# GEGLU feed-forward on one core: the first loads and the first products in another order

## The chip, the cores and the metric

One Trainium2 chip, one of its cores. The metric is the device time of one execution in microseconds (us); lower is better. Engines: TensorE (PE, its weight loads PEld), VectorE (DVE), ScalarE (ACT), GpSimd (POOL), and SyncE (SP), which here only issues DMAs. ScalarE issues DMAs too; "ACTq" and "SPq" are the issues of the two.

## The reference

x is 2048 x 1024, w_gate and w_up are 1024 x 3584, w_down is 3584 x 1024, all bfloat16:

```
def _gelu(x):
    return jax.nn.gelu(x, approximate=True)

def reference(x, w_gate, w_up, w_down):
    return (_gelu(x @ w_gate) * (x @ w_up)) @ w_down
```

## The kernel before

The tokens are worked in two halves of 1024 (`NH`), each in two token blocks of 512 (`TB`). x is needed transposed: `xT[tb]` holds 8 row blocks (`KD`, index kd) of 128 features by 512 tokens. For each half the 28 feature chunks of 128 columns are taken in 14 pairs (`pair_quads`); gate and up products of a pair are made with fewer matmuls through sums and differences of blocks (`s_sum`, `t_sum`, a Strassen-Winograd scheme), and `down_group` does the same for w_down. gelu is on ScalarE, the product of gate and up on VectorE.

The very first pair of the first half is different, since neither x nor the weights are on the chip: `first_pair_units` multiplies directly, row block by row block (`part`, which calls `mm_gu`, L264). `j` is 0 for gate and 1 for up, `u` is the chunk of the pair. Token block 0 comes first, so its first products need only the first row blocks of x and of the weights:

- Row blocks 0 to 3 of x for token block 0 are loaded as they lie (`load_x0`; a "quarter" is two row blocks, 256 KB) and transposed on TensorE (`transpose_x0`, L308): quarter 0 gives blocks 0 and 1, quarter 1 gives blocks 2 and 3. They are copied out of PSUM by VectorE (L316), block 3 by ScalarE (L318).
- Row blocks 4 to 7, and the whole of token block 1, come through DMA transposes on SyncE's queue (`load_xT`, L171).
- The weights' first 256 columns (`FA`) are loaded in row blocks 0-1, 2-4 and 5-7 for gate and for up (`load_w`, L160), before the other columns. A row block of these is 64 KB.

Until the first x is there, TensorE runs `NWARM` = 7 matmuls on constants (`warm`, L202), and one more of half the width as a filler between the first transposes and the first products.

The order on each engine is written out by hand: `sp`, `act`, `dve`, `pool` and `pe` chain each instruction behind the last one on the same engine, so the order of the calls is the order on the engine and on its DMA queue. ScalarE's DMA issues, its table load (`preload_act_table`, L225) and its copies are thus in one line. The build gives DMA completions eight semaphores in turn, so that each DMA waits, on the issuing engine, for the landing of the DMA that stands eight before it in the order of issue. Before the change these waits are, in ScalarE's queue: gate rows 5-7 for the second half of x quarter 0, up rows 5-7 for x quarter 1.

Later, `x_fill` loads token block 0 of the second half from a transposed copy in DRAM, in two DMAs of 512 KB.

Of the kernel before, what the change touches and what calls it, by code (L numbers as in the profile page):

```python
# [34 lines left out]
def kernel(  # L35
# [8 lines left out]
    nc = tc.nc  # L44
    P = 128
# [4 lines left out]
    KD = D // P  # L50
    KH = KD // 2
    KF = F // P
    TB = 512
# [7 lines left out]
    TSB = TB // P  # L61
    XQ = 256
    NXQ = D // XQ
    KPQ = XQ // P
# [41 lines left out]
    banks = [psum.tile([P, TB], F32, name=f"bank{i}") for i in range(8)]  # L106
    PB, VB, QB, RB = (0, 1), (2, 3), (4, 5), (6, 7)
    last_on = {}

    def on(engine, inst):  # L110

        if engine in last_on:
            tc.add_manual_dep(
                inst.ins, last_on[engine].ins.name, SCHED_DEP, reason="engine order"
            )
        last_on[engine] = inst
        return inst

    def sp(inst):
        return on("sp", inst)  # L120
# [18 lines left out]
    def pe(inst):  # L139
        return on("pe", inst)  # L140
# [3 lines left out]
    chunks = {}  # L144
# [10 lines left out]
    def load_w(key, j, k0, k1, queue=sp, f0=0, f1=FG):  # L155

        c0 = key[1] * FG
        eng = nc.scalar if queue is act else nc.sync
        src = (wgv, wuv)[j][:, k0:k1, c0 + f0 : c0 + f1]
        queue(eng.dma_start(out=chunks[key][j][:, k0:k1, f0:f1], in_=src))  # L160

    def load_x0(q, queue, ts0=0, ts1=TSB):
        eng = nc.scalar if queue is act else nc.sync
        cols = slice(q * XQ, (q + 1) * XQ)
        src = x2[ts0 * P : ts1 * P, cols].rearrange("(ts p) d -> p ts d", p=P)
        queue(eng.dma_start(out=xs0[:, ts0:ts1, cols], in_=src))

    def load_xT(xT, h, tb, k0, k1):
        t0 = h * SH + tb * TB
        sp(  # L170
            nc.sync.dma_start_transpose(  # L171
                out=xT[tb][:, k0:k1, :],
                in_=xv[t0 : t0 + TB, k0:k1, :],
            )
        )

    def new_x(tb):
        xT[tb] = xT_pool.tile([P, KD, TB], BF16, name=f"xT{tb}")

    xT = [None] * NTB  # L180
# [4 lines left out]
    FA = 2 * P  # L185
    first = (0, 0)
    load_x0(0, sp, 0, 2)
    load_x0(0, act, 2, TSB)
    load_w(first, 0, 0, 2, sp, 0, FA)
    load_x0(1, act)  # L190
    load_w(first, 1, 0, 2, sp, 0, FA)
    load_w(first, 0, 2, 5, act, 0, FA)
    load_w(first, 1, 2, 5, sp, 0, FA)
    ident = const_pool.tile([P, P], BF16, name="ident")
    make_identity(nc, ident[:])

# [3 lines left out]
    def warm(bank, n=TB):  # L200
        pe(
            nc.tensor.matmul(  # L202
                banks[bank][:, 0:n],
                lhsT=warm_l,
                rhs=warm_r[:, 0:n],
                start=True,
                stop=True,
            )
        )
# [4 lines left out]
    load_xT(xT, 0, 0, KH, KH + 1)  # L214
    behind_transpose = last_on["sp"]
    load_xT(xT, 0, 0, KH + 1, KH + 2)
    for j in range(2):
        load_w(first, j, 5, KD, act, 0, FA)
        tc.add_manual_dep(
            last_on["act"].ins,  # L220
            behind_transpose.ins.name,
            SCHED_DEP,
            reason="engine order",
        )
# [16 lines left out]
    def t_sum(name, c0=0, c1=KH):  # L241
        def b(j, l):
            return xT[l][:, j * KH + c0 : j * KH + c1, :]

        t0 = ("t1", "t2", "t3", "b22", "t4").index(name) * KH * TB
        t = t_mem[:, t0 : t0 + KH * TB].rearrange("p (a b) -> p a b", b=TB)
        tsum[name] = t
        t = t[:, c0:c1, :]
        if name == "b22":
            for c in range(c1 - c0):  # L250
                act(nc.scalar.copy(out=t[:, c, :], in_=b(1, 1)[:, c, :]))
            return
        in0, in1 = {
            "t1": lambda: (b(0, 1), b(0, 0)),
            "t2": lambda: (b(1, 1), tsum["t1"].bitcast(F32)[:, c0:c1, :]),
            "t3": lambda: (b(1, 1), b(0, 1)),
            "t4": lambda: (b(1, 0), tsum["t2"].bitcast(F32)[:, c0:c1, :]),
        }[name]()
        dve(nc.vector.tensor_tensor(out=t, in0=in0, in1=in1, op=ALU.subtract))  # L259


    def mm_gu(ps, w_sb, fi, tb, kd):
        pe(
            nc.tensor.matmul(  # L264
                ps[:],
                lhsT=w_sb[:, kd, fi * P : (fi + 1) * P],
                rhs=xT[tb][:, kd, :],
                start=(kd == 0),
                stop=(kd == KD - 1),
            )  # L270
        )

# [23 lines left out]
    def unit_out(hT, bset, fi, tb):  # L296
        mult(hT, gelu(banks[bset[0]]), banks[bset[1]], fi, tb)

    def transpose_x0(q):

        parts = [(2 * q, 0, 4), (2 * q + 1, 0, 4)]
        if q == 0:
            parts = [(0, 0, 2), (0, 2, 4), (1, 0, 4)]
        for n, (kd, ts0, ts1) in enumerate(parts):
            tp = banks[(PB + QB)[(2 * q + n) % 4]][:].bitcast(BF16)
            for ts in range(ts0, ts1):
                pe(
                    nc.tensor.transpose(  # L308
                        tp[:, ts * P : (ts + 1) * P],
                        xs0[:, ts, kd * P : (kd + 1) * P],  # L310
                        ident[:],
                    )
                )
            cols = slice(ts0 * P, ts1 * P)
            if q == 0 or n == 0:
                dve(nc.vector.tensor_copy(out=xT[0][:, kd, cols], in_=tp[:, cols]))  # L316
            else:
                act(nc.scalar.copy(out=xT[0][:, kd, cols], in_=tp[:, cols]))  # L318

    def part(held, tb, k0, k1, us=(0, 1), js=(0, 1)):  # L320
        for kd in range(k0, k1):
            for j in js:
                for u in us:
                    mm_gu(banks[held[u][j]], chunks[first][j], u, tb, kd)

    def first_pair_units(hT):

        held = (VB, RB)
        transpose_x0(0)
        warm(RB[1], TB // 2)  # L330
        part(held, 0, 0, KPQ, js=(0,))
        transpose_x0(1)
        part(held, 0, 0, KPQ, js=(1,))
        part(held, 0, KPQ, KD)
        t_sum("t1", 0, KH // 2)
        t_sum("t1", KH // 2, KH)
        for u in range(2):
            unit_out(hT, held[u], u, 0)
        held = (QB, PB)
        part(held, 1, 0, KH)  # L340
        t_sum("t2")
        t_sum("b22")
        t_sum("t3", 0, KH // 2)
        part(held, 1, KH, KD, (0,))
        unit_out(hT, held[0], 0, 1)
        t_sum("t3", KH // 2, KH)
        part(held, 1, KH, KD, (1,))
        unit_out(hT, held[1], 1, 1)
        for j in range(2):
            s_sum(0, 1, j, "s3", True, False)  # L350
        for name in ("s1", "s2", "s4"):
            for j in range(2):
                s_sum(0, 1, j, name)
# [284 lines left out]
    def x_rows(k0, k1):  # L638
        return x_dram[k0:k1, :, :].rearrange("k p t -> p k t")
# [242 lines left out]
    for h in range(NH):  # L882
# [83 lines left out]
        if h + 1 < NH:  # L966
            nh = h + 1
            new_x(0)

            def x_fill():  # L970
                for k0, k1 in ((0, KH), (KH, KD)):
                    src = x_rows(k0, k1)
                    sp(nc.sync.dma_start(out=xT[0][:, k0:k1, :], in_=src))

            def w_fill(c, j):
                if j == 0:
                    new_chunk((nh, c))
                for k0 in range(0, KD, KH):
                    load_w((nh, c), j, k0, k0 + KH)

            def s_fill(j, *names):
                for name in names:
                    s_sum(nh, 0, j, name, True)

            then0["m6"] = [x_fill]
            then1["m6"] = [lambda: w_fill(0, 0)]
            then1["m7"] = [lambda: w_fill(0, 1)]
            then1["m2"] = [
                lambda: s_fill(0, "s1"),
                lambda: s_fill(1, "s1"),  # L990
                lambda: s_fill(0, "s2"),
                lambda: s_fill(1, "s2"),
                lambda: s_fill(0, "s3"),
                lambda: s_fill(1, "s3"),
            ]
            then1["m3"] = [lambda: t_sum("t1")]
            then1["m4"] = [
                lambda: s_fill(0, "a22"),
                lambda: s_fill(1, "a22"),
                lambda: t_sum("b22"),  # L1000
                lambda: t_sum("t2"),
                lambda: t_sum("t3"),
                lambda: s_fill(0, "s4"),
                lambda: s_fill(1, "s4"),
                lambda: t_sum("t4"),
                pool_behind_dve,
                lambda: [w_fill(1, j) for j in range(2)],
            ]
# [32 lines left out]
```

## Time and profile before

| | us |
|---|---|
| median of 5 runs | 539.63 |
| lowest and highest run | 539.58, 540.7 |
| the profiled execution, its own time | 539.1 |
| its span on the core | 537.3 |

| engine | busy, us | share of the span |
|---|---|---|
| TensorE matmul | 531.7 | 99% |
| TensorE weight load | 377.8 | 70% |
| VectorE | 363.0 | 68% |
| ScalarE | 263.3 | 49% |
| GpSimd | 243.1 | 45% |

A line of the timeline or of the chain reads: start in us from the span's start, duration in us, engine, line of the kernel, operation, out<-in, count, and in brackets the idle time of the engine just before and what ended it. "issue" in the chain is time in which nothing that the profile shows was waited for. Several instructions of one kind in a row are merged into one line, with the time from the first's start to the last's end. In the view by windows the columns after the engines are the granted TensorE clock, the mean busy share of the 16 DMA engines, and GB/s moved.

### The profile page before, as it was taken

The page shows a single profiled execution, that of the slowest core. Times are in us where ns is not written, and L with a number is a line of the kernel's source. Part 1 is how long each engine was busy: PE and PEld are TensorE (multiplying, and loading weights), DVE is VectorE, ACT ScalarE, POOL GpSimd, SP SyncE. Part 2 cuts the span into 40 slices and gives each one's busy share as a digit, 9 for nine tenths or more (in the row PEclk, how much of TensorE's full clock was granted, in tenths as well). Part 3 has the DMA queues.
Part 4 walks back from the last instruction along what each step waited for, and adds up shares of the span by engine and source line. Part 5 has one row for each costly group of instructions (what it writes and reads, how often), then busy time and mean ns, then how long its engine had stood idle before and what let it go on. Part 6 is the DMA issues. An engine that isn't in the chain of part 4 may idle for free.

```text
span 537.3 us, 7084 instructions
## 1 busy us (share of the span) xinstructions
PE 531.7 (99%) x2352; PEld 377.8 (70%) x2388; DVE 363.0 (68%) x476; ACT 263.3 (49%) x447; POOL 243.1 (45%) x212
## 2 busy tenths in 40 slices
PE   9999999999999999999999999999999999999997
PEld 4577776667776686777776677777777766866866
DVE  2988767778775997989674334444444469969961
ACT  2655555555555329117465555555555551452280
POOL 0699877777776000000066776667777730000000
PEclk9999999999999999999999999999999999999999
DMA  9946876697816967789940405042222448677846
GB/s 216 324 124 196 213 240 203 219 211 250 293 60 208 357 237 263 230 284 298 329 163 1 157 1 158 19 139 67 91 78 80 157 137 281 228 244 246 291 143 212
DMA packets 92547, 102.70 MB, mean 191 GB/s; under 512 B 18656, under 2 KB 67424, under 8 KB 92512
## 3 DMA queue, kind: packets, MB, share of 16 engines
q1 hardware_dynamic: 69568, 80.23, 46.4%
q10 hardware_dynamic: 22944, 22.02, 13.5%
q8 instruction: 19, 0.31, 0.3%
q14 instruction: 16, 0.13, 0.1%
HBM read 85.98 MB, written 12.58 MB: 183 GB/s over the span
## 4 chain that ended last, share of the span: by engine, by line
PE 99%; issue 0%; ACT 0%; ACTq 0%
PE bank L413 63%; PE bank L703 33%; PE bank L264 3%; PE bank L202 1%; PE bank L308 0%; ACT bank L468 0%; ACT o_sb L759 0%; ACTq L468 0%
## 5 line engine op out<-in xcount | busy, mean ns | idle before, releaser
L413 PE MATMUL bank<-t_mem,s_mem 128*128 128x512 f32 x1056 | 249.4, 394 | 0.0
L413 PEld LDWEIGHTS bank<-t_mem,s_mem 128*128 128x128 f32 x1056 | 198.2, 188 | 43.8 <-ACT bank L464 0.2
L385 POOL TENSOR_TENSOR s_mem<-w_mem 128x512 fp32r<-128x512 bf16 x102 | 119.9, 1199 | 191.2 <-DVE t_mem L259 102.7
L703 PE MATMUL bank<-t_mem,s_mem 128*128 128x512 f32 (+1 forms) x548 | 127.2, 391 | 0.0
L288 DVE TENSOR_TENSOR hT<-w_mem,bank 128x512 bf16<-128x512 f32 x104 | 71.2, 686 | 81.0 <-PE bank L413 45.7
L703 PEld LDWEIGHTS bank<-t_mem,s_mem 128*128 128x128 f32 x548 | 102.5, 188 | 22.0
L436 DVE TENSOR_TENSOR bank<-bank,m 128x512 f32<-128x512 f32 x108 | 69.9, 694 | 45.3 <-ACT m L458 43.6
L413 PE MATMUL bank<-xT,w_mem 128*128 128x512 bf16 x405 | 96.5, 380 | 1.4
L283 ACT ACTIVATE w_mem<-bank 128x512 f32<-128x512 f32 x104 | 61.8, 597 | 52.1 <-DVE bank L436 35.6
L413 PEld LDWEIGHTS <-w_mem 128*128 128x128 bf16 x432 | 40.2, 98 | 51.6 <-issue 6.8
L385 POOL TENSOR_TENSOR s_mem<-w_mem,s_mem 128x512 fp32r<-128x512 bf16 x52 | 65.7, 1290 | 0.0
L605 DVE TENSOR_TENSOR t_mem<-w_mem 128x1024 fp32r<-128x1024 bf16 x56 | 65.5, 1217 | 0.0
L385 POOL TENSOR_TENSOR s_mem<-s_mem,w_mem 128x512 fp32r<-128x512 f32 x52 | 60.8, 1195 | 0.0
L464 ACT COPY bank<-bank 128x512 f32<-128x512 f32 x54 | 30.8, 570 | 38.9 <-PE bank L413 38.9
L398 ACT CAST s_mem<-w_mem 128x512 fp32r<-128x512 bf16 x54 | 33.1, 615 | 31.5 <-PE bank L413 30.1
L675 DVE TENSOR_TENSOR s_mem<-hT 128x512 fp32r<-128x512 bf16 x52 | 34.2, 685 | 10.2 <-PE bank L703 9.4
L458 ACT COPY m<-bank 128x512 f32<-128x512 f32 x54 | 31.8, 589 | 17.5 <-PE bank L413 17.5
L703 PEld LDWEIGHTS <-hT 128*128 128x128 bf16 x224 | 21.3, 98 | 26.6 <-issue 2.1
L468 ACT COPY bank<-bank 128x512 f32<-128x512 f32 x54 | 30.7, 570 | 12.2 <-PE bank L413 12.2
L630 DVE TENSOR_TENSOR o_sb<-wd_sb,o_sb 128x512 fp32r<-128x512 bf16 x28 | 31.7, 1132 | 0.5
L768 ACT CAST o_sb<-bank 128x512 bf16<-128x512 f32 x27 | 14.8, 585 | 33.8 <-PE bank L703 33.8
L602 ACT CAST t_mem<-w_mem 128x1024 fp32r<-128x1024 bf16 x28 | 26.9, 1047 | 0.0
(45 smaller groups left out, 236.4 us busy)
## 6 DMA issues: line engine op xcount, KB each, us to landing
t_mem<-t_dram SPq DMA_DIRECT2D x56, 512.0 KB, 5.1
w_mem<-in_w_gate_dram ACTq DMA_DIRECT2D x10, 1024.0 KB, 5.3
w_mem<-in_w_up_dram ACTq DMA_DIRECT2D x10, 1024.0 KB, 5.5
wd_sb<-in_w_down_dram SPq DMA_DIRECT2D x28, 256.0 KB, 4.3
t_dram<-o_sb SPq DMA_DIRECT2D x28, 256.0 KB, 3.0
wd_sb<-in_w_down_dram SPq DMA_DIRECT2D x12, 512.0 KB, 7.7
w_mem<-in_w_down_dram SPq DMA_DIRECT2D x4, 1024.0 KB, 6.5
w_mem<-in_w_down_dram SPq DMA_DIRECT2D x8, 512.0 KB, 8.3
```

What stands on the lines that cost most here:

```text
L283: act(nc.scalar.activation(out=g_sb, in_=ps[:], func=ACT.Gelu_apprx_tanh))
L288: nc.vector.tensor_tensor(out=hT[:, fc, tb * TB : (tb + 1) * TB], in0=g_sb, in1=ps[:], op=ALU.mult,)
L385: pool(nc.gpsimd.tensor_tensor(out=t, in0=in0, in1=in1, op=op))
L398: act(nc.scalar.copy(out=t, in_=a(1, 1)))
L413: nc.tensor.matmul(banks[bank][:], lhsT=lhs[:, c, :], rhs=rhs[:, c, :], start=start and c == 0, stop=c == KH - 1, skip_group_check=True,)
L436: nc.vector.tensor_tensor(out=banks[dst][:], in0=banks[src][:], in1=m5[j][:], op=ALU.add)
L458: act(nc.scalar.copy(out=m5[j][:], in_=banks[V_[j]][:]))
L464: act(nc.scalar.copy(out=banks[RB[j]][:], in_=banks[QB[j]][:]))
L605: dve(nc.vector.tensor_tensor(out=t, in0=in0, in1=in1, op=ALU.subtract))
L630: dve(nc.vector.tensor_tensor(out=t, in0=in0, in1=in1, op=ALU.subtract))
L675: dve(nc.vector.tensor_tensor(out=t, in0=in0, in1=in1, op=op))
L703: nc.tensor.matmul(banks[bank][:, c0:c1], lhsT=lhs(i, u), rhs=rhs(i)[:, c0:c1], start=start and i == 0, stop=stop and i == NS - 1, skip_gr ...
```

## The change

The second x quarter is loaded in two halves by tokens, the first on ScalarE's queue and the second on SyncE's, where it stands before the up rows 0-1. Gate rows 2-4 stay on ScalarE's queue, now ahead of the point where the up loads are issued; up rows 2-4 go from SyncE's queue to ScalarE's, before gate and up rows 5-7. The filler matmul is gone; the gate products of row block 0 are made in two halves of 256 tokens each (the first half has `start`, the second writes other columns of the same bank). For row blocks 2 and 3 the gate products of both blocks come before the up products of both. `x_fill` is one DMA of 1 MB.

The waits for completion semaphores that the build gives ScalarE's queue are then: up rows 2-4 for the second half of x quarter 0, gate rows 5-7 for the first half of x quarter 1, up rows 5-7 for gate rows 2-4. The table load and the copy of row block 3 follow behind these issues, as before.

```
     load_x0(0, sp, 0, 2)
     load_x0(0, act, 2, TSB)
     load_w(first, 0, 0, 2, sp, 0, FA)
-    load_x0(1, act)
+    load_x0(1, act, 0, 2)
+    load_x0(1, sp, 2, TSB)
+    load_w(first, 0, 2, 5, act, 0, FA)
     load_w(first, 1, 0, 2, sp, 0, FA)
-    load_w(first, 0, 2, 5, act, 0, FA)
-    load_w(first, 1, 2, 5, sp, 0, FA)
...
     load_xT(xT, 0, 0, KH + 1, KH + 2)
-    for j in range(2):
-        load_w(first, j, 5, KD, act, 0, FA)
+    for j, k0, k1 in ((1, 2, 5), (0, 5, KD), (1, 5, KD)):
+        load_w(first, j, k0, k1, act, 0, FA)
         tc.add_manual_dep(
...
         transpose_x0(0)
-        warm(RB[1], TB // 2)
-        part(held, 0, 0, KPQ, js=(0,))
+        for t0 in (0, TB // 2):
+            for u in range(2):
+                pe(
+                    nc.tensor.matmul(
+                        banks[held[u][0]][:, t0 : t0 + TB // 2],
+                        lhsT=chunks[first][0][:, 0, u * P : (u + 1) * P],
+                        rhs=xT[0][:, 0, t0 : t0 + TB // 2],
+                        start=t0 == 0,
+                        stop=False,
+                        skip_group_check=True,
+                    )
+                )
+        part(held, 0, 1, KPQ, js=(0,))
         transpose_x0(1)
         part(held, 0, 0, KPQ, js=(1,))
-        part(held, 0, KPQ, KD)
+        for j in range(2):
+            part(held, 0, KPQ, KH, js=(j,))
+        part(held, 0, KH, KD)
...
             def x_fill():
-                for k0, k1 in ((0, KH), (KH, KD)):
+                for k0, k1 in ((0, KD),):
                     src = x_rows(k0, k1)
                     sp(nc.sync.dma_start(out=xT[0][:, k0:k1, :], in_=src))
```

More of the change, by code (lines that the diff above doesn't have):

```diff
@@ L329, in first_pair_units @@
         transpose_x0(0)
-        warm(RB[1], TB // 2)
-        part(held, 0, 0, KPQ, js=(0,))
+        for t0 in (0, TB // 2):
[7 more added lines that the diff above has]
+                        stop=False,
+                        skip_group_check=True,
+                    )
+                )
+        part(held, 0, 1, KPQ, js=(0,))
         transpose_x0(1)
         part(held, 0, 0, KPQ, js=(1,))
-        part(held, 0, KPQ, KD)
+        for j in range(2):
+            part(held, 0, KPQ, KH, js=(j,))
+        part(held, 0, KH, KD)
         t_sum("t1", 0, KH // 2)
```

## The prediction

> **What bounds the kernel now.** I read the page first, then the chain that ended last in order of time, then the first 20 us engine by engine, then the DMA issues one at a time. The page's busy shares and the chain's head:
>
> ```profile
> PE 531.7 (99%) x2352; PEld 377.8 (70%) x2388; DVE 363.0 (68%) x476; ACT 263.3 (49%) x447; POOL 243.1 (45%) x212
> ...
> 0.73 0.04 issue
> 0.77 3.14 PE bank L202 x7
> 3.92 0.84 PE bank L308 x8
> 4.76 0.11 PE bank L202
> 4.87 1.00 PE bank L264 x4
> 5.87 0.45 PE bank L308 x8
> 6.31 4.59 PE bank L264 x21
> 10.90 0.05 issue
> 10.96 8.36 PE bank L264 x38
> ```
>
> TensorE is the chain from its first matmul to 534.4 us. From 10.96 on a 512-column product takes 8.36 / 38 = 0.22 us, and no later piece is a wait of any size. So the time changes only through what the edited opening (before about 12 us) does to TensorE's stream, and a delay there reaches the end unshortened: no idle time is left behind it in which to win it back. In the opening, narrow windows of the timeline put the filler at 4.60, the gate products of row block 0 at 4.82, of row block 1 at 5.27, the second transposes at 5.70, the up products of blocks 0 and 1 at 6.15, block 2 at 7.01, block 3 at 7.88, block 4 at 8.74, block 6 at 10.53 instead of 10.46 (0.07 us lost).
>
> The three things that feed this stream are VectorE's copies, ScalarE's queue and the transfers:
>
> ```profile
> 4.21 1.01 DVE L316 COPY xT<-bank 128x256 bf16<-128x256 bf16 x3 [4.21 <-PE bank L308]
> 6.13 0.42 DVE L316 COPY xT<-bank 128x512 bf16<-128x512 bf16 x1 [0.91 <-PE bank L308]
> ```
>
> ```profile
> 0.73 1.03 ACTq L166 DMA_DIRECT2D w_mem<-in_x_dram  x2
> 1.79 2.62 ACTq L160 DMA_DIRECT2D w_mem<-in_w_gate_dram  x2
> 5.35 0.38 ACTq L160 DMA_DIRECT2D w_mem<-in_w_up_dram  x1
> 5.76 1.28 ACT L225 ACT_TABLE_LOAD   x1 [5.76 <-DMA w_mem<-in_x_dram]
> 7.05 0.59 ACT L318 COPY xT<-bank 128x512 bf16<-128x512 bf16 x1
> ```
>
> The second of these fences is the one to look at. ScalarE issues its DMAs, loads its table and only then makes the copy at L318, which is row block 3 of x. That copy ends at 7.64 and TensorE takes it up at 7.88, with 0.19 us to spare (0.05 us from a copy's end to the product, as from 5.22 to 5.27 behind VectorE's third copy). The DMA view of single issues (columns: transfer, queue, count, KB, us from issue to landing):
>
> ```profile
> w_mem<-in_x_dram ACTq DMA_DIRECT2D x1, 256.0 KB, 4.1
> w_mem<-in_w_gate_dram ACTq DMA_DIRECT2D x1, 192.0 KB, 5.1
> w_mem<-in_w_up_dram SPq DMA_DIRECT2D x1, 128.0 KB, 4.0
> w_mem<-in_w_up_dram SPq DMA_DIRECT2D x1, 192.0 KB, 4.9
> ```
>
> With their issue times: the second x quarter lands at 1.25 + 4.1 = 5.35, up rows 0-1 at 1.75 + 4.0 = 5.75, gate rows 2-4 at 1.79 + 5.1 = 6.9, up rows 2-4 at 2.25 + 4.9 = 7.15. The last up load of ScalarE's queue is issued at 5.35, the moment the x quarter lands: eight completion slots go round, and the built program makes each DMA wait for the landing of the eighth before it. The gate load issued at 4.02 shows the same (ScalarE's first x half was issued at 0.73 and took 3.3).
>
> **The change, part by part.**
>
> *Filler out, half-width products in.* The filler (0.22 us, 4.60 to 4.82) goes, and the two 512-column gate products of block 0 become four of half the width: no net work. The first pair needs only VectorE's first copy (4.21 + 0.29 = 4.50), so it starts at 4.60; the second pair needs the copy that ends at 4.77 and starts at 4.82. Then block 1 needs the third copy, which ends at 5.22 whatever TensorE did. So it starts at 5.27, as before: gain 0. Bounds: 0, and 0.22 if that copy were out of the way.
>
> *Second x quarter in two halves.* ScalarE takes token blocks 0-1, SyncE 2-3, and SyncE's half stands before up rows 0-1. Transposes want it at 5.70 (second half 5.81). At worst it lands where up rows 0-1 did (5.75, the same third place on SyncE), at best with 128 KB less ahead of it, 5.3. Either way in time: 0. The DMA engines are already full here:
>
> ```profile
> 4.00:5.00 1.00, 1.00 (x10) 0.74 (x9) 0.76 (x3) 0.00 (x0) 0.00 (x0) 1.00 1.20 320
> 5.00:6.00 1.00, 1.00 (x10) 0.58 (x9) 0.22 (x1) 0.24 (x1) 0.00 (x0) 1.00 1.13 289
> 6.00:7.00 1.00, 1.00 (x10) 0.48 (x8) 0.42 (x1) 1.00 (x1) 0.00 (x0) 1.00 1.27 236
> ```
>
> The last two columns are their share (over 1) and GB/s; a reordering moves one transfer forward by moving another back, 128 KB for 0.45 us at 289 GB/s. The Trainium skill, DMA: Bandwidth & Descriptors, section "Issuing engines are not separate DMA queues", has a rule against this part: DMAs of all issuing engines run on the same 16 DMA engines, so a second queue saves only issue time. By that rule alone the split would gain at most one issue, about 0.5 us, of a landing that nothing waits for, and the sum below would be the same.
>
> *Up rows 0-1 go fourth on SyncE.* Before them or beside them now stand both x quarters, gate 0-1 and gate 2-4: 960 KB with themselves, where it was 768 KB. 192 KB more at 289 GB/s is 0.68 us: they land at 5.79 + 0.68, about 6.45. TensorE wants them at 6.15, so the up products of blocks 0-1 start near 6.5 (0.35 lost). Bounds: 0 if they land by 6.15; 1.0 if as late as the fourth SyncE load before, 7.15.
>
> *Gate rows 2-4 move up, and ScalarE's copy moves back.* This is the term that decides. The added DMA shifts the slots: in the changed program the last up load of ScalarE's queue waits for gate rows 2-4, not for the x quarter, and the table load and the L318 copy are queued behind it on the same engine. Gate rows 2-4 have 832 KB up to and with them instead of 960 KB. From 768 KB at 5.79 that is 0.23 more, 6.0; from 960 KB at 6.9 it is 0.45 less, 6.45. I take the middle, 6.25, since both rows are 192-KB or 128-KB loads of the same stretch. From the awaited landing to the end of the copy it was 7.64 - 5.35 = 2.3 us (issue 0.38, table 1.28, copy 0.59 and gaps), so the copy ends near 8.55 and the product can start at 8.6.
>
> *Order of blocks 2 and 3.* Gate of 2, gate of 3, up of 2, up of 3, instead of alternating; so block 3's gate products are wanted 0.43 us sooner after the start of block 2 than before. From the up products at 6.5: 4 x 0.216 for them and 2 x 0.216 for block 2's gate, 7.8. TensorE then waits from 7.8 to 8.6, 0.8 us. This contains the 0.35 above; they don't add. From 8.6 six products (0.43 + 0.86) lead to block 4 at 9.9, where it was 8.74: 1.17 later. The old loss of 0.07 at block 6 vanishes, since its transposed x lands at 5.32 + 5.2 = 10.5 and is wanted at 11.6. **Sum: +1.10 us.** Bounds: gate rows 2-4 at 6.0 give +0.85, at 6.5 +1.35, and unmoved at 6.9 +1.75.
>
> *Up rows 2-4 on ScalarE's queue.* Issued at 4.02 instead of 2.25 (they now wait for the slot of ScalarE's first x half), in the place of the gate load that took 4.3: landing 8.3, wanted after block 3's gate products at 9.05. Cover 0.7; cost 0. The two loads behind: gate rows 5-7 issued near 4.9, landing near 9.5, wanted at 10.8; up rows 5-7 issued at 6.3, landing 10.6, wanted at 11.2 (0.6 to spare; if a 256-KB transpose gets in ahead, 256 KB at 257 GB/s is 1.0 and 0.4 is lost).
>
> *SyncE's transposes* keep fifth place, and the slots they wait for land no later: 0. *x_fill in one DMA:* issued at 204.6 and 205.1 with 6.1 to 7.6 us to landing, first wanted by VectorE at 263.5: over 50 us of cover, 0.
>
> The profiled execution took 539.1 us around a span of 537.3, and 540.2 is the sum on it; the five runs' median lies 0.5 us higher, 539.63, so I predict 540.73. Above or below 0.2%, 1.08 us, is about what a measurement of this kernel can tell from no change, and my sum lies on that line.
>
> **The rivals.** (a) *Not slower by the bound:* gate rows 2-4 land early. Place: the wait of ScalarE's last DMA issue; price: 1 us for 1 us; the point is 6.23 us, below it the loss is under 1.08. For it: most of the 16 engines should be done well before the slowest, and 6.0 is the estimate from the nearer byte count. Against: the same load took 5.1 us, the longest of its neighbours, and the whole load has to land. It gives +0.5 to +1.08, about 540.5. (b) *No stall at all:* only if ScalarE's copy ended by 7.4, so if gate rows 2-4 landed by 5.1, before the x quarter did; then the filler and the 0.07 are the gain, at most 0.29, 539.35, still within the bound. A larger gain has no place: at 19.88 a weight load just gets its up rows (a 0.19 us wait). (c) *More goes wrong:* up rows 5-7 late (0.4), rows 2-4 unmoved (1.75), or TensorE's clock. The row: the seven first matmuls took 3.14 us, 0.45 each against 0.22 later, though the page grants 1.00 in every slice. A second such stretch of 3.1 us costs 3.14 - 7 x 0.22 = 1.6 more. The Trainium skill, TensorE: Matmul & The Clock Gate, says that only an idle gap of some 3 us brings the slow clock back; by it the waits here (0.35 and 0.8) would cost nothing more. Together +1.5 to +2.7, about 541.6.
>
> **How the numbers follow.** My forecast (+1.08 to +1.5) 0.42; (a) 0.41; (b) 0.03; (c) 0.12; a gain of over 1.08 from something the trace doesn't show 0.02. Slower by over 0.2%: 0.42 + 0.12 = 0.54. Within: 0.41 + 0.03 = 0.44. Faster 0.02. The range, 540.1 to 541.5, is +0.5 to +1.9: it holds the forecast, (a) and half of (c), 0.9 at most, and the gate rows' bounds of 6.0 to 6.9.
>
> **What would show it.** Right: ACT_TABLE_LOAD at 6.6 to 6.9 instead of 5.76, the L318 copy (its line is 319 then) ending at 8.4 to 8.7, a TensorE wait for ACT of 0.6 to 1.0 before block 3, block 4 near 9.9, all later stages shifted by 1.0 to 1.2. A wait for up rows 0-1 at 6.15 of 0.2 to 0.5. Wrong: the table load near 5.8 (the slot argument fails, and the loss is under 0.5), block 1 before 5.2 (the filler did cost), matmuls spaced 0.43 after 5 us (the clock), or a stall behind block 4 (up rows 5-7).

## The result

| | before | changed |
|---|---|---|
| median of the runs, us | 539.85 (40 runs) | 541.08 (22 runs) |
| lowest and highest, us | 539.17, 541.69 | 540.18, 541.72 |
| the profiled execution, us | 539.1 | 540.93 |
| its span, us | 537.3 | 539.1 |

The ratio of the changed kernel to the one before is 1.0019, 95% interval 1.0012 to 1.0025: slower by 1.0 us (0.65 to 1.35). The difference of the medians is 1.23 us. The profiled executions lie 1.8 us apart, more than the runs: that of before, and a second one of 539.27, lie at the fast end of that kernel's runs, those of the changed kernel (540.93, and a second one of 541.46) near the middle of its own.

The changed kernel's page, and then the part of its chain in order of time that answers to the one shown of before (start, length, engine, what):

```profile
PE 532.1 (99%) x2353; PEld 378.2 (70%) x2389; DVE 363.3 (67%) x476; ACT 263.2 (49%) x447; POOL 244.9 (45%) x212
```

```profile
4.02 4.71 DMA xT<-in_x_dram
8.73 0.58 ACT xT L319
9.32 0.04 issue
9.36 3.41 PE bank L264 x15
12.77 0.05 issue
12.82 8.37 PE bank L264 x38
```

Busy times are nearly what they were. The chain no longer runs through TensorE from the first matmul: it comes to it from ScalarE's copy (L319, L318 before), which ends at 9.30. That the view puts a DMA transpose ahead of the copy, landed at 8.73, is a coincidence of times: in the second profile of this kernel the copy starts at 8.69, before that transpose lands (8.79), and in both it starts 0.01 us behind the end of the table load. The piece of 38 products, the same in both kernels, starts at 12.82 instead of 10.96. From its start to the end of the span it is 526.3 us in both, so all of the difference is made before it, as the prediction had it, and the single `x_fill` DMA costs nothing. I call this start **the mark**; in the fourteen profiles here the span is the mark plus 526.3 to 526.8.

ScalarE's timeline, from 3 us on:

```profile
3.63 0.37 ACTq L160 DMA_DIRECT2D w_mem<-in_w_up_dram  x1
5.56 0.41 ACTq L160 DMA_DIRECT2D w_mem<-in_w_gate_dram  x1
6.99 0.41 ACTq L160 DMA_DIRECT2D w_mem<-in_w_up_dram  x1
7.43 1.28 ACT L225 ACT_TABLE_LOAD   x1 [7.43 <-DMA w_mem<-in_w_gate_dram]
8.72 0.58 ACT L319 COPY xT<-bank 128x512 bf16<-128x512 bf16 x1
```

The last up load is issued at 6.99, when gate rows 2-4 land at 1.79 + 5.2; the table load and the copy follow. The bracket of the table load names that load. TensorE's timeline shows who waits:

```profile
5.23 0.79 PE L334 MATMUL bank<-xT,w_mem 128*128 128x256 bf16 x4 [0.46 <-DVE xT L317]
...
7.09 1.47 PE L264 MATMUL bank<-xT,w_mem 128*128 128x512 bf16 x6 [0.20 <-DMA w_mem<-in_w_up_dram]
9.36 0.38 PE L264 MATMUL bank<-xT,w_mem 128*128 128x512 bf16 x1 [0.80 <-ACT xT L319]
```

Three waits. The third is the predicted one: block 3's gate product starts at 9.36, 1.18 us behind the product before it, where 0.22 is the spacing, so 0.96 is lost. The second is the predicted wait for up rows 0-1 (7.09 instead of 6.73: 0.36). The first was not foreseen. The bracket names VectorE's copies, but the one that the first product needs ended at 4.46; the waits of the weight loads name gate rows 0-1, which landed at 5.2 here and at 4.44 before.

### The profile page after: what moved, and what is told of

The parts are those of the page before. It is cut to its first block, busy times and chain, and to the rows that moved or that the text cites. A ratio compares the mean times of both kernels' runs of the same rounds, so it can differ in the third digit from the quotient of the medians.

```text
span 539.1 us, 7081 instructions
## 1 busy us (share of the span) xinstructions
PE 532.1 (99%) x2353; PEld 378.2 (70%) x2389; DVE 363.3 (67%) x476; ACT 263.2 (49%) x447; POOL 244.9 (45%) x212
## 4 chain that ended last, share of the span: by engine, by line
PE 97%; DMA 1%; SPq 1%; issue 0%; ACT 0%; ACTq 0%
PE bank L427 63%; PE bank L717 33%; PE bank L264 2%; DMA xT<-in_x_dram 1%; SPq L171 0%; SPq L160 0%; SPq L166 0%; ACT xT L319 0%; ACT bank L482 0%; ACT o_sb L773 0%; ACTq L482 0%
```

## The experiments

Ratios are to the kernel before, run beside them on the same chip. "B" is an edit of the kernel before, "A" of the changed kernel. Each has eleven runs, the copy on VectorE five.

**A, unedited, again.**

> The changed kernel unedited, for a second profile. Its first profile is 1.8 us longer in span than the profile of before, the runs only 1.2 (medians). Theory (ScalarE's last DMA issue waits for gate rows 2-4, and the table load and the copy of row block 3 stand behind it): the wait for ScalarE before block 3 comes back, 0.8 to 1.2 us, and the run is 0.8 to 1.3 us over before. Rival (the reordered transfers themselves come late: gate rows 0-1 landed at 5.2 instead of 4.4 in the first profile): the wait of 0.6 us before the first half-width products comes back as well, in the same size. If the theory alone holds for most executions, that first wait is 0 to 0.2 us here.

Ratio 1.0020 (1.0011 to 1.0029), span 539.7, mark 13.12. Gate rows 2-4 land at 6.97 once more, the copy ends at 9.27, and TensorE loses 0.93 us before block 3. The wait at the first half-width products is there too, smaller: they start at 4.88 because gate rows 0-1 land at 4.83. So neither "0 to 0.2" nor "the same size": both things are real, and the second varies. Up rows 0-1 cost 0.81 us here, not 0.36: they land at 7.04 in both profiles, but TensorE is ready for them at 6.28. A new wait stands at block 5, 0.32 us, for up rows 5-7, which land at 12.20.

**A, the copy of block 3 on VectorE.**

```
-            if q == 0 or n == 0:
+            if True:
                 dve(nc.vector.tensor_copy(out=xT[0][:, kd, cols], in_=tp[:, cols]))
```

> The changed kernel, with the copy of row block 3 on VectorE instead of ScalarE. Theory: the wait of about 1 us before block 3 goes (VectorE's two copies end by 7.6), so the time is 0.8 to 1.0 us under the changed kernel, 0 to 0.4 us over before. Rival (late transfers): the wait moves to the up rows 2-4 or stays at the first products, and at most 0.3 us is won.

Ratio 1.0031 (1.0019 to 1.0044), span 540.4, mark 13.61: not faster at all, so the theory as I then had it falls (its profiled execution, 542.29, is the slowest of the five). The wait before block 3 is gone as expected. The chain in order of time says what took its place:

```profile
1.79 5.38 DMA w_mem<-in_w_gate_dram
7.17 0.02 issue
7.19 5.49 DMA w_mem<-in_w_up_dram
12.69 0.05 issue
12.73 0.82 PE bank L264 x3
```

Gate rows 2-4 land at 7.17, the last up load (rows 5-7) is issued at that moment, takes 5.49 us and is waited for at block 5. The wait for the slot holds two things back, the copy behind it on ScalarE and the transfer itself; the second is late by nearly as much as the first, and with the first cured it is the bound.

**A, the table load ahead of the last three DMA issues.**

```
+    act(nc.scalar.preload_act_table(ACT.Gelu_apprx_tanh))
     for j, k0, k1 in ((1, 2, 5), (0, 5, KD), (1, 5, KD)):
...
-    act(nc.scalar.preload_act_table(ACT.Gelu_apprx_tanh))
```

> The changed kernel, with ScalarE's table load ahead of its last three DMA issues (it then lies in 2.3 to 3.6, where ScalarE waits for the first x half anyway). The copy stays on ScalarE behind the issue that waits for gate rows 2-4. Theory: the copy ends 1.28 us sooner, near 7.5 to 8.0, and the wait before block 3 falls to 0 to 0.2 us: 0.8 to 1.0 us under the changed kernel. Rival (late transfers): no gain over 0.2 us.

Ratio 1.0017 (1.0008 to 1.0026), mark 13.18. The copy ends at 7.92 instead of 9.30 and the wait before block 3 is gone, but up rows 5-7, issued at 6.77, land at 12.26, and block 5 starts its up products at 12.30, 0.7 us late. What the issue waits for is another landing here: the built program goes round the completion slots in another order, and the last up load gets the slot of SyncE's half of the second x quarter, which came free at 6.75. Gate rows 2-4, at 7.63, are no longer waited for by ScalarE at all, and still the transfer is as late. The same exchange as with the copy, for another reason.

**A, blocks 2 and 3 in the old order.**

```
-        for j in range(2):
-            part(held, 0, KPQ, KH, js=(j,))
-        part(held, 0, KH, KD)
+        part(held, 0, KPQ, KD)
```

> The changed kernel, with gate and up products of blocks 2 and 3 alternating as before. Theory: ScalarE's copy ends when it did, but the two up products of block 2 (0.43 us) are done in the wait, if up rows 2-4 are there (landing 8.3): 0.43 us under the changed kernel, the wait before block 3 0.4 to 0.7 us. Rival (the order of the products is the whole loss): back to before.

Ratio 1.0014 (1.0005 to 1.0023); the expected 0.43 us is 0.0008, and the measured step from 1.0020 is 0.0006, which the intervals don't separate. The profile is more telling than the ratio, because in this execution, the fastest of the eleven, gate rows 2-4 came early. ScalarE:

```profile
6.13 0.37 ACTq L160 DMA_DIRECT2D w_mem<-in_w_up_dram  x1
6.54 1.28 ACT L225 ACT_TABLE_LOAD   x1 [6.54 <-DMA w_mem<-in_w_gate_dram]
7.83 0.58 ACT L319 COPY xT<-bank 128x512 bf16<-128x512 bf16 x1
```

They landed at 6.11, the up load was issued at 6.13, and the copy ended at 8.41, by the 2.3 us of the prediction's term. The mark is 11.64. In the four profiles in which that wait is there, gate rows 2-4 landed at 6.11, 6.97, 6.97 and 7.17.

**A, up rows 5-7 on SyncE's queue.**

```
-    for j, k0, k1 in ((1, 2, 5), (0, 5, KD), (1, 5, KD)):
+    for j, k0, k1 in ((1, 2, 5), (0, 5, KD)):
...
+    load_w(first, 1, 5, KD, sp, 0, FA)
     load_xT(xT, 0, 0, KH + 2, KD)
```

> The changed kernel, with up rows 5-7 issued on SyncE's queue behind the second transpose, where their slot waits for gate rows 0-1; nothing on ScalarE's queue then waits for gate rows 2-4. Corrected theory: that one wait holds two things back, the copy of row block 3 and the up rows 5-7 themselves, so curing the copy alone moves the stall to block 5, and only an earlier issue cures both. It expects up rows 5-7 issued near 5.3 and landed by 10.5, the copy ended by 8.0, no TensorE wait over 0.3 us at blocks 3 and 5, and a time 0.7 to 1.2 us under the changed kernel. Rival (late landings by themselves, stragglers among the DMA engines): the stall stays somewhere between block 0 and block 6, and less than 0.3 us is won.

Ratio 1.0010 (1.0002 to 1.0019), span 538.1, mark 11.50. The table load is at 5.05 and the copy ends at 7.23; up rows 5-7 are issued at 5.32 and land at 10.20. The chain is TensorE's own again:

```profile
6.62 0.01 issue
6.62 4.83 PE bank L265 x21
11.45 0.05 issue
```

Two small waits are left, 0.16 us for up rows 0-1 at 6.62 and 0.12 at block 6, for the DMA transpose that now stands behind one load more. In the profile, which is that of the fastest of the eleven runs, the gain is 1.3 to 1.6 us (mark 11.50 against 12.82 and 13.12; 0.7 to 1.2 was expected); in the runs it is 0.0009 to 0.0010 under the changed kernel, 0.5 us, and the intervals overlap.

**The same with blocks 2 and 3 in the old order.** (Both edits above.)

> The changed kernel with up rows 5-7 on SyncE's queue behind the second transpose, and gate and up products of blocks 2 and 3 alternating as before. Corrected theory: with nothing waiting for gate rows 2-4 only the later up rows 0-1 are left of the loss, 0.1 to 0.5 us over before, 0.6 to 1.0 under the changed kernel; no wait at block 3. Rival (the split of the x quarter is the loss): 0.7 us or more over before, with waits before block 2.

Ratio 1.0005 (0.9997 to 1.0014), which can't be told from before; the unedited changed kernel had 1.0011 to 1.0029. No wait at block 3. Its profile, though, has the mark at 12.18: gate rows 0-1 land at 4.95, up rows 0-1 at 6.95, and up rows 2-4, issued at 3.69, at 8.67, each with a wait of TensorE behind it. So with the wait for the slot gone the runs come back to within what they can tell from before, though the split of the x quarter is still there; single executions still meet late landings.

**A, the x quarter whole again.**

```
-    load_x0(1, act, 0, 2)
-    load_x0(1, sp, 2, TSB)
+    load_x0(1, act)
```

> The changed kernel with the second x quarter whole again, on ScalarE's queue: one DMA less, so up rows 2-4 wait for no slot, gate rows 5-7 wait for the x quarter, and up rows 5-7 for gate rows 0-1. Corrected theory: up rows 5-7 issued near 5.7 and landed by 10.8, the copy ended by 8.1; waits of 0 to 0.4 us before block 3 and none at block 5: 0.6 to 1.0 us under the changed kernel. Rival (the order of products and the up rows on ScalarE's queue are the loss): less than 0.3 us is won.

Ratio 1.0016 (1.0007 to 1.0025), mark 11.99. Up rows 5-7 were issued at 5.74 and landed at 11.07, which cost TensorE 0.08 us. But the issue took 0.75 us, the table load began at 6.51 and the copy ended at 8.39, so block 3 still lost 0.52 us. In the profile 0.8 to 1.1 us is won against the changed kernel, in the runs nothing that the intervals resolve. Inconclusive.

**B, the split of the x quarter alone, on two queues and on one.**

```
-    load_x0(1, act)
+    load_x0(1, act, 0, 2)
+    load_x0(1, sp, 2, TSB)
```

> The kernel before with the x quarter in two halves on the two queues and nothing else: up rows 0-1 go fourth on SyncE, and the slot waits fall on early landings (gate rows 5-7 for the first x half, up rows 5-7 for gate rows 0-1). Corrected theory: the split by itself costs the later landing of up rows 0-1 alone, a TensorE wait of 0.2 to 0.5 us before their first products; 0.1 to 0.5 us over before. Rival (the split is what makes the first landings late): waits of over 0.6 us at the first products and the second transposes, and as slow as the changed kernel.

```
-    load_x0(1, act)
+    load_x0(1, act, 0, 2)
+    load_x0(1, act, 2, TSB)
```

> The kernel before with the x quarter in two halves, both on ScalarE's queue, so up rows 0-1 keep the third place on SyncE. Slot waits: the first transpose now waits for SyncE's first x half, up rows 5-7 for gate rows 0-1. Theory (the place of the up rows costs, not the split): no wait before the first up products, the same time as before within 0.3 us. Rival (two half loads make the DMA engines drift apart, and the slowest engine sets each landing): a spread of over 0.8 us at gate rows 0-1, waits at the first products or at block 2, and 0.5 us or more over before.

On two queues: ratio 1.0016 (1.0008 to 1.0025), more than expected. No slot waits for gate rows 2-4 here, the copy ends at 7.62 in good time, and yet the mark is 12.04. Up rows 0-1, fourth on SyncE, landed at 7.24, and TensorE waited for them from 6.83 to 7.28; SyncE's x half, landed at 6.44, had cost it 0.16 us; the rest of the lateness is the slow clock (below). On one queue: ratio 1.0012 (1.0003 to 1.0020), against an expected zero. Here I had overlooked a cost of the added DMA: the first transpose is now the ninth and waits for ScalarE's first x half, landed at 3.85 (the expectation names the wrong half). It is issued at 3.86 instead of 2.77 and lands at 9.90, and block 4 waits for it until 9.94. So neither run prices the split without the shift of the slots. By the runs alone the split on two queues, 1.0016, can't be told from the whole change, 1.0019; what speaks against it as the cause is the run of both edits above, which has the split and 1.0005.

**B, the half-width products alone.**

```
-        warm(RB[1], TB // 2)
-        part(held, 0, 0, KPQ, js=(0,))
+        for t0 in (0, TB // 2):
...
+        part(held, 0, 1, KPQ, js=(0,))
```

> The kernel before with the filler replaced by the half-width products and nothing else. Prediction: block 1 waits for VectorE's third copy in both, so the same time within 0.1 us. Rival (the filler cost its 0.22 us): 0.2 us under before, block 1 starting before 5.2.

Ratio 1.0004 (0.9995 to 1.0013): the same time, as predicted; a gain of the filler's whole 0.22 us (0.9996) is just within the interval. The start of block 1, 5.47 here, can't decide, for the reason told at the end.

**B, a second table load.**

```
+    act(nc.scalar.preload_act_table(ACT.Exp))
     act(nc.scalar.preload_act_table(ACT.Gelu_apprx_tanh))
```

> The kernel before with a second table load (of another function) on ScalarE ahead of the one it has; nothing else. It prices a delay of ScalarE's copy of row block 3 by itself. Theory (1 us for 1 us beyond the slack of 0.19 us, all later work shifted): the copy 1.28 us later, TensorE waits 1.1 us before block 3, and the time is 0.9 to 1.2 us over before, ratio 1.0017 to 1.0022. Rival (the copy's lateness is not what the changed kernel loses by; lost time is won back behind it): ratio under 1.0010.

The chain shows exactly the wait that was built:

```profile
6.86 1.28 ACT L226
8.14 0.01 issue
8.15 0.59 ACT xT L319
8.74 0.04 issue
8.79 2.97 PE bank L265 x13
```

The mark is 11.80, the span 538.3, 0.8 to 1.0 us over the two profiles of before. The runs gave 1.0009 (1.0000 to 1.0018), half of what was expected, though the rival's "under 1.0010" is met by its middle alone. How the runs lie tells more: they go from 540.04 to 540.82, those of the kernel before, run beside them, from 539.06 to 541.92. The fast end moved by 1.0 us, the median by 0.34. I read it so (argued, not shown): the copy's time hangs on landings and not on TensorE, so it is a floor under the mark; an execution in which TensorE is late anyway loses less by it.

**B, unedited, again.**

> The kernel before, unedited, for a second profile of it. The matmul spacing in the profiles so far falls from the slow to the fast rate at 4.5 us in the profile of before, and at 5.4 to 6.0 in those of the variants, among them the half-width variant that is no slower in the runs. If that moment differs from execution to execution whatever the kernel, it lies anywhere from 4.5 to 6.5 here, and the span follows it by up to 0.8 us; if it is the kernel's doing (filler, order), it is 4.5 again and the span 537.3. Gate rows 0-1 should land with 0.3 to 0.8 us between the first and the last DMA engine, as in the other profiles with the x quarter whole.

Ratio 0.9993 (0.9984 to 1.0002), span 537.5, mark 10.80. The matmul spacing halves at 4.1 us, in the first profile of this kernel at 4.5: just outside the 4.5 to 6.5 expected, but not the same either (more on this at the end). Gate rows 0-1 landed at 4.48, with 0.8 us between the first DMA engine and the last.

No version ran faster than the kernel before.

## Why the prediction was right, step by step

The forecast was +1.10 us with a range of +0.5 to +1.9; the runs give 1.0 by the ratio and 1.2 by the medians.

- *The slot wait on gate rows 2-4, and the table load and copy behind it:* right, and the main loss. From landing to the copy's end 9.30 - 6.97 = 2.33 us, forecast 2.3. The wait before block 3 was 0.96, forecast 0.8.
- *The landing of gate rows 2-4:* mis-sized. I took 6.25, with 6.0 to 6.5 as near bounds and 6.9 as the far one; four profiles show 6.11 to 7.17, three of them near 7. I had worked it out from the bytes ahead of it, as if the 16 DMA engines finished together. In the changed kernel's profile the first engine had finished at 5.20, the last at 6.97; in the profile of before 6.09 and 6.92. The bytes moved the first engine's end, the last one's hardly. Block 4 started at 10.65, forecast 9.9.
- *Up rows 0-1:* the size of the wait was right (0.36, forecast 0.35) by luck, two errors of 0.6 us that cancel: they landed at 7.04 instead of 6.45, and TensorE was ready at 6.73 instead of 6.15. In the second profile it was 0.81.
- *Up rows 5-7:* wrong. I gave them 4.3 us from issue to landing and 0.6 us of cover; they took 4.6 to 5.5 us, behind an issue that itself was mostly 0.7 later, and landed at 11.90, 12.20 and 12.69 (10.72 in the profile where the gate rows came early). In the changed kernel that hides almost wholly under the wait before block 3; the two runs that removed the latter brought it out. I had it among the things that "go wrong" at 0.4, when it is the second half of the main mechanism.
- *The second x quarter:* forecast 5.3 to 5.75, in time. Its halves landed at 5.54 and 6.24 in the changed kernel's profile; TensorE wanted them at 6.29 only because it was late already. "Either way in time" did not hold: with the copy on VectorE and with the split alone the second half landed at 6.23 and 6.44, and TensorE lost 0.50 and 0.16 us by it. By the rule of the Trainium skill (DMA: Bandwidth & Descriptors, "Issuing engines are not separate DMA queues") the second queue could save issue time only. The run of the split alone agrees: 1.0016, no landing that mattered came sooner.
- *Filler and half-width products:* 0 forecast, 1.0004 (0.9995 to 1.0013) measured.
- *Gate rows 0-1:* not in the prediction at all. They are unmoved on SyncE's queue, but landed at 5.2 and 4.83 in the two profiles of the changed kernel, at 4.44 and 4.48 before. In the chain of these profiles it costs nothing more, because the later waits cover it.
- *Up rows 2-4 on ScalarE's queue:* right. Forecast 8.3 and 0 cost; they landed at 8.39 and nothing waited. With both edits above, where they are wanted sooner, landing at 8.67 cost 0.41.

The mechanism was right but for the late up rows 5-7, and so was the size of the main wait (0.96 and 0.93); the times that the prediction named for it were all too early: the table load came at 7.43 (6.6 to 6.9 forecast), the copy ended at 9.30 (8.4 to 8.7), the stages behind were shifted by 1.86 (1.0 to 1.2). Two of its signs of being wrong came as well: the slow matmul spacing, until about 5.6 us, and in the second profile a stall of 0.32 behind block 4.

So that the number fits is in part luck. Gate rows 2-4 came later than forecast, which adds: the profiled execution lost 1.8 us, close to the bound of 1.75 that the prediction gave for gate rows unmoved at 6.9. The runs as a whole lost 1.0 to 1.2. I read the difference as executions in which TensorE is late anyway and so loses less; that is argued from the run with two table loads, not shown. Rival (a), gate rows early, is the execution in the run with the old order (6.11). Rival (b) happened nowhere. Of rival (c) the late up rows were real. The slow clock did not come back: once the spacing has halved it stays at 0.22 in all fourteen profiles, through waits of TensorE of up to 1.6 us. It did last longer in some executions, as told below.

Two things stay open. The runs separate the ends of the row (the changed kernel from before, and hardly the changed kernel with both edits) but not each step between: single steps are 0.3 to 0.5 us, an interval of eleven runs is 0.5 us to either side. And why gate rows 0-1 land later with the split on two queues: the first and the last DMA engine were 0.2 to 1.5 us apart on them in the eight profiles with that split (over 0.7 in six), 0.2 to 0.8 in the six others, which is a hint and no proof.

## What to carry to other kernels

When a DMA is added, count the completion slots again and ask, for each issue behind it, whose landing it now waits for and what is queued behind that issue on its engine: here one extra DMA moved a wait from one landing to a later one, and a table load, a copy and a transfer moved with it. When two things hang on one wait, curing one shows only the other; price both before building a fix. A landing is the time of the last DMA engine, so work it out from the slowest of several rows and not from bytes.

## What the runs showed of the hardware that was not expected

**When TensorE's fast rate begins.** The matmul spacing halves at one moment early in each execution, and that moment is not the kernel's doing. TensorE's timeline of the changed kernel at the first transposes, in its first profile and then in its second:

```profile
3.71 1.06 PE L309 MATMUL bank<-ident,w_mem 128*128 128x128 bf16 x8
```

```profile
3.71 0.65 PE L309 MATMUL bank<-ident,w_mem 128*128 128x128 bf16 x8
```

The same eight transposes of the same kernel start at the same time and take 1.06 us in the one execution and 0.65 in the other: the spacing halves at 5.6 us in the first and at 3.8 in the second. In the fourteen profiles the moment lies between 3.5 us (the run with two table loads) and 6.6 (the table load first), while the first matmul starts at 0.77 or 0.78 in all of them. The profile's column of the granted clock says 1.00 throughout, but it counts time without a record as full: the clock records in the traces (the changed kernel's first profile has none) begin at just these moments, 4.51 and 4.12 us in the two profiles of the kernel before, 3.78 in the changed kernel's second. The first record, at full clock, is 532.48 us long in nine of the thirteen traces and 535.89 in four. The two differ by 3.41 us, and are 156 and 157 times 3.413. The Trainium skill, TensorE: Matmul & The Clock Gate, Part 1, says that the window which releases the clock is free-running and 3413 ns long, and does not reset when a kernel starts; the lengths of the records, and a spread of the moment of 3.1 us from one execution to the next, agree with that window. The spread does not agree with the ±500 ns that the page gives for the moment itself. By estimate, 2.1 us more at half the rate than in the profile of before (6.6 against 4.5) delays TensorE by about 1 us where no wait covers it, so two profiles of an opening like this one are not compared before this moment is looked up in both.

**Around the first DMA transpose the packets of both queues end together.** The windows view of the changed kernel (last two columns: DMA share, GB/s):

```profile
5.00:6.00 1.00, 0.77 (x5) 0.58 (x6) 0.23 (x1) 0.00 (x0) 0.00 (x0) 1.00 1.88 275
6.00:7.00 1.00, 0.90 (x11) 0.53 (x8) 0.29 (x1) 0.00 (x0) 0.00 (x0) 1.00 0.71 133
```

A packet is counted in the window in which it starts. Those that start between 5 and 6 us keep the engines busy for longer than before (1.88, where it was 1.13), and in the next microsecond 133 GB/s start instead of 236. In the trace 22 packets of both queues, SyncE's and ScalarE's, start one after another from 5.6 us on and all end between 6.71 and 6.77: the longest takes 1.15 us, where 0.03 is usual. In the profile of before such packets start at 6.6 and take 0.2 to 0.3 us. All fourteen profiles have one such joint end, 0.7 to 2.0 us behind the start of the first transpose's packets (256 bytes on SyncE's queue), and it is latest (8.2 and 7.7 us) in the two runs of the split alone, which issue that transpose latest (3.57 and 3.86 instead of 2.3 to 2.8). It looks as if every engine waits until the last one is through the transpose, so that one engine that lags costs all of them; no run isolates this.
